# Retention and a gated two-layer product on one core: the queries of the sixth to eighth piece loaded as squares

## The chip, the cores and the metric

The kernel runs on one core of a Trainium2 chip. The metric is the device time of one execution in microseconds (us), and a kernel's time is the median of several executions. The engines are TensorE (PE: matmuls; PEld: the loading of their weights), VectorE (DVE), ScalarE (ACT), GpSimd (POOL) and SyncE (SP, which here only issues DMAs). Each engine works through its own instructions in the order in which the program gives them.

## The reference, cut to what matters

```python
# q, k, v: (B=8, H=8, S=576, D=64) float32; w_in (512, 2048), w_out (2048, 512) float64
scores = q @ k.transpose(0, 1, 3, 2) / sqrt(64)
gamma = 1 - 2.0 ** (-5 - arange(8))                     # one decay for each head
Dmat = where(i >= j, gamma ** (i - j), 0)               # i: query's place, j: key's place
ret = (scores * Dmat) @ v
x = ret.transpose(0, 2, 1, 3).reshape(4608, 512)
h = x @ w_in                                            # (4608, 2048)
out = (h * erf(softplus(h))) @ w_out                    # (4608, 512)
```

## The kernel before

**Pieces and chunks.** The 4608 tokens are cut into 36 pieces of 128 tokens (`pieces`). Nine pieces hold two sequences: four of the first, four of the second, and one with the last 64 tokens of both. Pieces are counted from 0 in the code, so the "sixth to eighth" are pieces 5, 6 and 7, the second to fourth piece of the second sequence. Four pieces (`PC = 4`) make a chunk of 512 tokens, and the two-layer product works on one chunk at a time.

**The retention of a piece** is three steps. `transposes(i)` brings the queries and keys into the form that TensorE needs, with the head's 64 dimensions on the partitions (`qT`, `kT`). `scores(i)` makes 8 products `s` of `kT` and `qT` (L347), which VectorE multiplies by the triangular mask into `sT` (L99, two instructions of 128x512). `outputs(i)` makes the outputs `o` from `sT` and the values (L365), adds what the sequence's running state gives (L376), and forms the new state from keys and values (L388). VectorE scales `o` into the chunk's operand `x` (L99), and the state is decayed (L427). The values are weighed by the keys' decay on GpSimd (`weigh_values`, L313).

**Two forms of loading.** `load_rows` reads a piece of q, k or v with tokens on the partitions, in two DMAs of 128 KB made of runs of 256 bytes (L147). Queries and keys loaded so are transposed by TensorE, four 128x128 transposes against `ident` into PSUM (L332), and copied out by ScalarE (L334 for q, L338 for k). `load_squares` reads a piece in four DMAs, one for each 32 partitions, with runs of 896 bytes (L131). VectorE then transposes all squares of 32x32 in one instruction (L326, `STREAM_TRANSPOSE`), with no TensorE and no ScalarE in it. Each of the four DMAs is 112 KB, because every run covers four tokens, of which half the dimensions are used. In the kernel before, queries are squares from piece 8 (`SQUARES = 2 * PC`) and keys from piece 12, unless the piece is one of those that need the keys with tokens on the partitions; those have rows of k as well.

**The weights** come as 64-bit floats. `round_weights` turns them into 32-bit floats part by part, four parts for the first group of `w_in` (`wa`): two steps on ScalarE (L254, L255), then six on VectorE (L259, L263, L267, L272, L274, L275) one behind the other; for other parts the last two are on GpSimd.

**The two-layer product** is made of products by 7 sums in place of 8 (`First`, `Second`), but for the first two chunks, whose first layer is made plainly (`plain`, L550: tiles `p`, `pe`, `pg`, which need the four parts of `wa` one after the other).

**Order.** Everything is put in order by hand. The beginning, with the first chunk's retention, the rounding and the first plain products, follows a string of letters: `a` is the next step of the retention, `p` a quarter of a plain product, a digit that many rounding steps, `w` the loading of a weight part, `k` two filler products.

```python
    keep_busy(10)
    ...
    for what in "alkakakawkakakawaa3awwa2aaa5ppappawwppa5ppapp5wawcppa5ppappaa5s":
```

Loads are issued ahead: `transposes(i)` ends with the queries of piece i + 2, and `outputs(i)` ends with keys and values of piece i + 3. All go to SyncE's queue, but the keys of piece 0, which go to ScalarE's. A tile framework puts a wait ahead of each instruction for what it reads and overwrites; its DMAs take 8 completion semaphores in turn, so a DMA is issued only after the one 8 places ahead of it has landed.

**Filler products.** `keep_busy(n)` issues n products of a tile with itself, whose result is not used: ten at the start, and two at each `k`. The tile is `ones`, which VectorE fills.

Of the kernel before, what the change touches and what calls it, by code (L numbers as in the profile page):

```python
# [11 lines left out]
FP32 = mybir.dt.float32  # L12
# [6 lines left out]
P = 128  # L19
# [35 lines left out]
def kernel(  # L55
# [10 lines left out]
    nc = tc.nc  # L66
# [15 lines left out]
    cpool = ctx.enter_context(tc.tile_pool(name="cpool", bufs=1))  # L82
# [18 lines left out]
    def flat(ap):  # L101
        return ap.rearrange("p h d -> p (h d)")

    heads = [slice(e * D, (e + 1) * D) for e in range(2)]
# [7 lines left out]
    PC = TCH // P  # L112
# [3 lines left out]

    SQUARES = 2 * PC
    SQUARES_K = 3 * PC  # L120
    SQ = 32

    def load_squares(i, name, src):
        t = raw.tile([P, NP, P * D // SQ], FP32, tag=name + "s", name=f"raw_{name}s", bufs=2)
        for b, s0, n, r0 in pieces[i]:
            m = n // SQ * D
            for part in range(P // SQ):
                e, d0 = part // 2, part % 2 * SQ
                tokens = src[b, e * NP : (e + 1) * NP, s0 : s0 + n, :].rearrange("p (r a) d -> r p (a d)", r=SQ)
                at = r0 // SQ * D  # L130
                nc.sync.dma_start(  # L131
                    out=t[part * SQ : (part + 1) * SQ, :, at : at + m - SQ], in_=tokens[:, :, d0 : d0 + m - SQ]
                )
        return t

    def load_rows(i, name, src, bufs):
        if name == "q":
            t = raw.tile([P, NP, P * D // SQ], FP32, tag="qs", name="raw_q", bufs=bufs)
            t = t.rearrange("p a x -> p (a x)")[:, : H * D].rearrange("p (h d) -> p h d", h=H)
        else:  # L140
            t = raw.tile([P, H, D], FP32, tag=name, name=f"raw_{name}", bufs=bufs)
        for b, s0, n, r0 in pieces[i]:
            for e in range(2):
                heads = src[b, e * NP : (e + 1) * NP, s0 : s0 + n, :]

                queue = nc.scalar if (name, i) == ("k", 0) else nc.sync
                queue.dma_start(out=t[r0 : r0 + n, e::2, :], in_=heads.rearrange("h p d -> p h d"))  # L147
        return t

    def load(i, names="qkv"):  # L150
        if i < len(pieces):
            t = loaded.setdefault(i, {})
            for name in names:
                src = {"q": q, "k": k, "v": v}[name]
                if name == "q" and i < SQUARES:
                    t["q"] = load_rows(i, "q", q, 2)
                elif name == "q":
                    t["qs"] = load_squares(i, "q", q)
                    if i >= SQUARES_K:
                        t["ks"] = load_squares(i, "k", k)  # L160
                elif name == "v" or i < SQUARES_K or len(pieces[i]) == 1:
                    t[name] = load_rows(i, name, src, 4)

    ones = cpool.tile([P, P], FP32, name="ones")
    nc.vector.memset(ones, 1.0)
    load(0)
    cst = cpool.tile([P, CONST_COLS], FP32, name="cst")
    nc.sync.dma_start(out=cst[:, :CONST_FIRST], in_=consts[:, :CONST_FIRST])
# [123 lines left out]
    ident = cpool.tile([P, P], FP32, name="ident")  # L292
# [21 lines left out]

    def transposes(i):
        t = live[i] = loaded.pop(i)
        if i < SQUARES:
            weigh_values(i)
        for name in "qk":
            tT = t[name + "T"] = att.tile([P, NP, P], FP32, tag=name + "T", name=name + "T")  # L320
            if name + "s" in t:
                for _, _, n, r0 in pieces[i]:
                    a = r0 // SQ * D
                    squares = t[name + "s"][:, :, a : a + n // SQ * D].rearrange("p h (a d) -> p h a d", d=D)
                    order = "p h (a r) -> p h a r" if name == "q" else "p h (r a) -> p h a r"
                    nc.vector.transpose(  # L326
                        out=tT[:, :, r0 : r0 + n].rearrange(order, r=SQ), in_=squares[:, :, :, :SQ]
                    )
            else:
                pt = ps_at.tile([P, NP, P], FP32, tag="at", name=f"pt_{name}")  # L330
                for p in range(NP):
                    nc.tensor.transpose(pt[:, p, :], flat(t[name][:, 2 * p : 2 * p + 2, :]), ident)  # L332
                if name == "q":
                    nc.scalar.copy(  # L334
                        out=tT.rearrange("p h (a r) -> p h a r", r=SQ), in_=pt.rearrange("p h (r a) -> p h a r", r=SQ)
                    )
                else:
                    nc.scalar.copy(out=tT, in_=pt)  # L338
        load(i + 2, "q")
# [14 lines left out]
    def outputs(i):  # L354
        segments = pieces[i]
        t = live.pop(i)
        seen = [(kept[b], r0, n) for b, s0, n, r0 in segments if s0 > 0]

        b, s0, n, _ = segments[0]
        o = [ps_at.tile([P, NP, P], FP32, tag="at", name=f"o{j}") for j in range(2)]
        for p in range(NP):
            for e in range(2):
                nc.tensor.matmul(  # L365
                    o[p % 2][heads[(e + p) % 2], p // 2, :],
                    lhsT=t["v"][:, 2 * p + e, :],
                    rhs=t["sT"][:, e, p, :],
                    start=(p < 2),
                    stop=(not seen and p >= NP - 2),  # L370
                    skip_group_check=True,
                )
        for state, r0, m in seen:
            for p in range(NP):
                for e in range(2):
                    nc.tensor.matmul(  # L376
                        o[p % 2][heads[(e + p) % 2], p // 2, r0 : r0 + m],
                        lhsT=state[heads[e], p, :],
                        rhs=t["qT"][heads[e], p, r0 : r0 + m],
                        start=False,  # L380
                        stop=(p >= NP - 2),
                        skip_group_check=True,
                    )
        if n == P:
            kv = flat(o[0])[:, 2 * P :].rearrange("p (a d) -> p a d", a=NP)
            for p in range(NP):
                for e in range(2):
                    nc.tensor.matmul(  # L388
                        kv[heads[e], p, :],
                        lhsT=t["k"][:, 2 * p + e, :],  # L390
                        rhs=t["v"][:, 2 * p + e, :],
                        start=False,
                        stop=(p == NP - 1),
                        skip_group_check=True,
                    )
        c, at = i // PC, i % PC * P
        if (0, c) not in x:
            x[0, c] = x_tile()

        def scaled(j):  # L400
            to = x[0, c][:, j:NP:2, at : at + P]
            if c < n_ch - 1:
                by = (gq if n == P else gq2)[:, j::2, :].unsqueeze(2).to_broadcast([P, 2, P // n, n])
                dst, got = (y.rearrange("p a (m i) -> p a m i", i=n) for y in (to, o[j][:, :2]))
                tt(dst, got, by, ALU.mult)
                return

            for r0 in range(0, P, n):
                dst = to[:, :, r0 : r0 + n].rearrange("p h (r a) -> p h a r", r=SQ)
                got, by = (  # L410
                    y.rearrange("p h (a r) -> p h a r", r=SQ)
                    for y in (o[j][:, :2, r0 : r0 + n], (gq if n == P else gq2)[:, j::2, :])
                )
                tt(dst, got, by, ALU.mult)

        scaled(1)
        if n == P:
            sums = kv
            if s0 > 0:
                sums = att.tile([P, NP, D], FP32, tag="sums", name="sums")  # L420
                tt(sums, kv, kept[b], ALU.add)

            if b % 2 == 0 and s0 + P + D == S:
                new = att.tile([P, NP, D], FP32, tag="last", name="last", bufs=1)
            else:
                new = att.tile([P, NP, D], FP32, tag="state", name="state")
            (nc.gpsimd if s0 > 0 else nc.vector).tensor_tensor(out=new, in0=sums, in1=gp, op=ALU.mult)  # L427
            kept[b] = new
        scaled(0)
        load(i + 3, "kv")  # L430
        if i + 1 >= SQUARES:
            weigh_values(i + 1)

    stages = [(transposes, 0), (scores, 0)]
# [271 lines left out]
    idle = ps_e.tile([P, W], FP32, tag="g", name="idle")  # L706

    def keep_busy(n):
        for _ in range(n):
            nc.tensor.matmul(idle[:, :P], lhsT=ones, rhs=ones, start=True, stop=True)  # L710


    most = [before_chunk(2)]
# [4 lines left out]
            attend(min(done[0] + stages, most[0]))  # L718
            round_weights(rounds[step] if step < len(rounds) else 0)

    keep_busy(10)
    weigh_values(0)
    products = firsts[0].plain()

# [36 lines left out]
    for b, nxt in zip(blocks[2:], blocks[3:] + [None]):  # L761
        n = order.index((b.g, b.c))
# [73 lines left out]
```

## Time and profile before

| | |
|---|---|
| median of 3 executions | 1028.51 us (1027.02 to 1029.08) |
| the profiled execution | 1028.51 us, of which the span of instructions is 1026.7 us |
| PE busy | 1017.5 us (99%), 6348 instructions |
| DVE busy | 669.2 us (65%) |
| ACT busy | 390.2 us (38%) |
| POOL busy | 123.5 us (12%) |
| the chain that ended last | PE 95%, DMA 2%, DVE 2% |
| DMA | 165.76 MB, mean 161 GB/s |
| granted TensorE clock | 1.00 |

Times in the trace are counted from the first instruction. A line such as `31.56 0.63 PE L332 MATMUL pt_q<-ident,raw_q ... x4 [0.24 <-DMA raw_q<-in_q_dram]` says: at 31.56 us TensorE began four instructions of line 332 that write `pt_q`; before them it had been idle for 0.24 us, until the DMA that writes `raw_q` landed. `SPq` lines are DMA issues on SyncE's queue. A TensorE instruction's duration includes its way through the array, and the next one starts earlier; the chain of waits shows the time that a group takes from the next.

### The profile page before, as it was taken

The page shows a single profiled execution, that of the slowest core. Times are in us where ns is not written, and L with a number is a line of the kernel's source. Part 1 is how long each engine was busy: PE and PEld are TensorE (multiplying, and loading weights), DVE is VectorE, ACT ScalarE, POOL GpSimd, SP SyncE. Part 2 cuts the span into 40 slices and gives each one's busy share as a digit, 9 for nine tenths or more (in the row PEclk, how much of TensorE's full clock was granted, in tenths as well). Part 3 has the DMA queues.
Part 4 walks back from the last instruction along what each step waited for, and adds up shares of the span by engine and source line. Part 5 has one row for each costly group of instructions (what it writes and reads, how often), then busy time and mean ns, then how long its engine had stood idle before and what let it go on. Part 6 is the DMA issues. An engine that isn't in the chain of part 4 may idle for free.

```text
span 1026.7 us, 15951 instructions
## 1 busy us (share of the span) xinstructions
PE 1017.5 (99%) x6348; PEld 876.0 (85%) x6348; DVE 669.2 (65%) x1055; ACT 390.2 (38%) x481; POOL 123.5 (12%) x122
## 2 busy tenths in 40 slices
PE   9999999999999999999999999999999999999998
PEld 8778888888788888888888888888888888888887
DVE  3868777877876666656666666666567655555555
ACT  2254134233134444434443344444443333333332
POOL 2143112122312110010001001000100000000000
PEclk9999999999999999999999999999999999999999
DMA  9999889979974344544445345444433334444333
GB/s 197 190 240 195 224 199 222 250 153 245 237 183 161 128 144 144 168 162 160 154 150 170 123 144 157 170 146 144 144 124 124 123 131 131 126 133 135 124 91 115
DMA packets 146986, 165.76 MB, mean 161 GB/s; under 512 B 97376, under 2 KB 121568, under 8 KB 138848
## 3 DMA queue, kind: packets, MB, share of 16 engines
q1 hardware_dynamic: 144848, 163.70, 56.3%
q10 hardware_dynamic: 2064, 1.05, 0.4%
q8 instruction: 50, 0.82, 0.4%
q14 instruction: 24, 0.20, 0.1%
HBM read 117.52 MB, written 47.19 MB: 160 GB/s over the span
## 4 chain that ended last, share of the span: by engine, by line
PE 95%; DMA 2%; DVE 2%; SPq 0%; issue 0%; ACT 0%; DVEq 0%
PE a L604 24%; PE a L496 23%; PE g L604 12%; PE g L496 12%; PE e L604 6%; PE e L496 6%; PE s L347 3%; PE o L365 3%; PE o L388 1%; PE o L376 1%; DMA raw_k<-in_k_dram 1%; PE p L550 1%; PE idle L710 1%; DMA wraw<-in_moe_w_out_dram 1%; PE pg L550 1%; PE pe L550 1%
## 5 line engine op out<-in xcount | busy, mean ns | idle before, releaser
L496 PE MATMUL a<-x,wa 128*128 128x256 f32 x1088 | 258.3, 380 | 0.0
L496 PEld LDWEIGHTS a<-x,wa 128*128 128x128 f32 x1088 | 205.7, 190 | 28.5
L604 PE MATMUL a<-wb,s 128*128 128x256 f32 x864 | 205.7, 381 | 0.0
L604 PEld LDWEIGHTS a<-wb,s 128*128 128x128 f32 x864 | 162.9, 190 | 23.6 <-ACT o L618 0.7
L99 DVE TENSOR_TENSOR t<-g,t 128x512 f32<-128x512 f32 x68 | 47.0, 691 | 150.9 <-ACT t L526 113.3
L496 PE MATMUL g<-x,wa 128*128 128x256 f32 x544 | 129.2, 380 | 0.0
L496 PEld LDWEIGHTS g<-x,wa 128*128 128x128 f32 x544 | 102.8, 190 | 14.4
L99 DVE TENSOR_TENSOR o<-a,o 128x512 f32<-128x512 f32 x108 | 74.1, 686 | 49.3 <-PE a L604 49.3
L521 ACT COPY t<-a 128x512 f32<-128x512 f32 x34 | 19.9, 586 | 188.2 <-PE a L496 188.2
L99 DVE TENSOR_TENSOR t<-t,s 128x1024 f32<-128x1024 f32 x72 | 89.4, 1282 | 0.0
L565 ACT ACTIVATE s<-t 128x1024 f32<-128x1024 f32 x72 | 72.2, 1049 | 27.3 <-DVE t L99 27.3
L274 POOL TENSOR_TENSOR wraw<-wraw 128x512 f32<-128x512 f32 x28 | 29.5, 1052 | 435.8 <-DVE wraw L272 187.0
L99 DVE TENSOR_TENSOR x<-x 128x512 f32<-128x512 f32 x115 | 75.8, 693 | 1.2
L532 ACT COPY t<-a 128x512 f32<-128x512 f32 x34 | 19.9, 587 | 144.4 <-PE a L496 144.4
L569 ACT ACTIVATE s<-s 128x1024 f32<-128x1024 f32 x72 | 72.1, 1049 | 0.4
L604 PE MATMUL g<-wb,s 128*128 128x256 f32 x288 | 68.6, 381 | 0.0
L604 PE MATMUL e<-wb,t 128*128 128x256 f32 x288 | 68.5, 380 | 0.0
L604 PE MATMUL a<-wb,t 128*128 128x256 f32 x288 | 68.5, 380 | 0.0
L604 PE MATMUL g<-wb,t 128*128 128x256 f32 x288 | 68.2, 380 | 0.0
L99 DVE TENSOR_TENSOR sT<-s,cst 128x512 f32<-128x512 f32 x72 | 46.2, 682 | 31.6 <-PE s L347 31.5
L99 DVE TENSOR_TENSOR o<-g,o 128x512 f32<-128x512 f32 x72 | 49.2, 684 | 24.5 <-ACT o L618 19.7
L496 PE MATMUL e<-x,wa 128*128 128x256 f32 x272 | 64.8, 381 | 0.0
(76 smaller groups left out, 1225.5 us busy)
## 6 DMA issues: line engine op xcount, KB each, us to landing
od<-o SPq DMA_DIRECT2D x54, 512.0 KB, 3.3
x<-xd SPq DMA_DIRECT2D x27, 1024.0 KB, 4.8
o<-od SPq DMA_DIRECT2D x27, 1024.0 KB, 5.3
raw_qs<-in_q_dram SPq DMA_DIRECT2D x96, 112.0 KB, 4.7
raw_ks<-in_k_dram SPq DMA_DIRECT2D x84, 112.0 KB, 4.1
xd<-x SPq DMA_DIRECT2D x9, 1024.0 KB, 5.2
raw_v<-in_v_dram SPq DMA_DIRECT2D x64, 128.0 KB, 4.7
wraw<-in_moe_w_in_dram SPq DMA_DIRECT2D x32, 256.0 KB, 5.9
```

The source lines that it names most:

```text
L99: nc.vector.tensor_tensor(out=out, in0=in0, in1=in1, op=op)
L274: engine.tensor_tensor(out=r_f, in0=high_f, in1=r_f, op=ALU.mult)
L347: nc.tensor.matmul(ps[e][:, p, :], lhsT=t["kT"][heads[e], p, :], rhs=t["qT"][heads[e], p, :], start=True, stop=True)
L365: nc.tensor.matmul(o[p % 2][heads[(e + p) % 2], p // 2, :], lhsT=t["v"][:, 2 * p + e, :], rhs=t["sT"][:, e, p, :], start=(p < 2), stop=(no ...
L376: nc.tensor.matmul(o[p % 2][heads[(e + p) % 2], p // 2, r0 : r0 + m], lhsT=state[heads[e], p, :], rhs=t["qT"][heads[e], p, r0 : r0 + m], s ...
L496: nc.tensor.matmul(acc[:, j * TH : (j + 1) * TH], lhsT=weights["wa", self.g][:, a, d, j * P : (j + 1) * P], rhs=x[self.g, self.c][a][:, d, :],
L521: nc.scalar.copy(out=self.t1[:, 1], in_=self.a)
L532: nc.scalar.copy(out=self.t2[:, 0], in_=self.a)
L550: nc.tensor.matmul(acc[n][:, j * TH : (j + 1) * TH], lhsT=wa[:, slots[f], dc % 2, j * P : (j + 1) * P], rhs=t[:, dc, tok * TH : (tok + 1) ...
L565: nc.scalar.activation(self.s[:, j], t, AF.Softplus)
L569: nc.scalar.activation(self.s[:, j], self.s[:, j], AF.Erf)
L604: nc.tensor.matmul(acc[:, tp, :], lhsT=left[:, j * TH + tp * P : j * TH + (tp + 1) * P], rhs=weights["wb", self.g][:, b, j, :], start=(sta ...
```

## The change

Queries become squares from piece 5 instead of piece 8 (keys as before from piece 12). The keys of piece 0 go to SyncE's queue, between the queries and the values of piece 0. The tile `ones` is gone: the filler products use `ident`, which GpSimd makes, and the first series has nine instead of ten. The two other uses of `SQUARES`, which say when the values are weighed, are written as `2 * PC` and keep their value.

```diff
-    SQUARES = 2 * PC
+    SQUARES_Q = PC + 1
     SQUARES_K = 3 * PC
...
-
-                queue = nc.scalar if (name, i) == ("k", 0) else nc.sync
-                queue.dma_start(out=t[r0 : r0 + n, e::2, :], in_=heads.rearrange("h p d -> p h d"))
+                nc.sync.dma_start(out=t[r0 : r0 + n, e::2, :], in_=heads.rearrange("h p d -> p h d"))
...
-                if name == "q" and i < SQUARES:
+                if name == "q" and i < SQUARES_Q:
                     t["q"] = load_rows(i, "q", q, 2)
...
-    ones = cpool.tile([P, P], FP32, name="ones")
-    nc.vector.memset(ones, 1.0)
...
-        if i < SQUARES:
+        if i < 2 * PC:
             weigh_values(i)
...
-        if i + 1 >= SQUARES:
+        if i + 1 >= 2 * PC:
             weigh_values(i + 1)
...
-            nc.tensor.matmul(idle[:, :P], lhsT=ones, rhs=ones, start=True, stop=True)
+            nc.tensor.matmul(idle[:, :P], lhsT=ident, rhs=ident, start=True, stop=True)
...
-    keep_busy(10)
+    keep_busy(9)
```

Line numbers after the change are lower by 2 to 4: the DMA of rows moves from L147 to L145, TensorE's transposes from L332 to L328, VectorE's from L326 to L322, the scores from L347 to L343, the masked scores stay on L99, the outputs move from L365 to L361, the plain product from L550 to L546.

## The prediction

> **What bounds the kernel now.** First the page, the share of each engine:
>
> ```profile
> PE 1017.5 (99%) x6348; PEld 876.0 (85%) x6348; DVE 669.2 (65%) x1055; ACT 390.2 (38%) x481; POOL 123.5 (12%) x122
> ```
>
> TensorE is busy 99% of the span, so a change is worth what it takes from TensorE's own work, less the idle time that it makes. Second, TensorE's waits over the whole span, to see how little there is:
>
> ```profile
> PE idle L710 <- DVE ones L165: 1.1, 1, 1.1
> PE s L347 <- DVE kT L326: 0.9, 1, 0.9
> PE o L365 <- POOL raw_v L313: 0.8, 1, 0.8
> PE p L550 <- DVE wa L275: 0.7, 1, 0.7
> PE pt_k L332 <- DMA raw_k<-in_k_dram: 0.7, 2, 0.4
> ```
>
> All but the second lie in the first 70 us, where the change is. Third, therefore, TensorE's timeline around pieces 5 and 6:
>
> ```profile
> 29.32 1.99 PE L550 MATMUL p<-x,wa 128*128 128x256 f32 x8
> 31.56 0.63 PE L332 MATMUL pt_q<-ident,raw_q 128*128 128x128 f32 x4 [0.24 <-DMA raw_q<-in_q_dram]
> 32.63 0.63 PE L332 MATMUL pt_k<-ident,raw_k 128*128 128x128 f32 x4 [0.44 <-DMA raw_k<-in_k_dram]
> ...
> 46.21 0.60 PE L332 MATMUL pt_q<-ident,raw_q 128*128 128x128 f32 x4
> 46.64 0.60 PE L332 MATMUL pt_k<-ident,raw_k 128*128 128x128 f32 x4
> 47.08 1.03 PE L550 MATMUL pe<-x,wa 128*128 128x256 f32 x4
> 47.95 1.03 PE L550 MATMUL pg<-x,wa 128*128 128x256 f32 x4
> 48.90 1.16 PE L347 MATMUL s<-qT,kT 64*128 64x128 f32 x16
> ```
>
> Piece 5 waits for its loads: TensorE runs here as fast as the DMAs allow. Piece 6 waits for nothing. Fourth, VectorE's timeline over the same time:
>
> ```profile
> 39.52 1.29 DVE L99 TENSOR_TENSOR sT<-s,cst 128x512 f32<-128x512 f32 x2 [2.24 <-PE s L347]
> 40.73 0.42 DVE L259 TENSOR_SCALAR wa<-wa 128x512 f32<-128x512 f32 x1
> ...
> 45.23 0.79 DVE L259 TENSOR_SCALAR wa<-wa 128x512 f32<-128x512 f32 x1
> ...
> 49.22 0.69 DVE L275 TENSOR_TENSOR wa<-wa,wraw 128x512 f32<-128x512 f32 x1
> 50.09 1.29 DVE L99 TENSOR_TENSOR sT<-s,cst 128x512 f32<-128x512 f32 x2 [0.18 <-PE s L347]
> ```
>
> From the masked scores of piece 5 (39.52) to the end of the last rounding step (49.22 + 0.69 = 49.91), VectorE has no gap: sT, the third part of `wa`, three scalings, the fourth part. It has 65% of the span, but none to spare here.
>
> **The change, part by part.** The sum is made on the profiled execution: 1028.51 us, 1.8 of it outside the span of 1026.7; it is also the median, so differences carry over unchanged.
>
> *TensorE's transposes go.* Three groups of four. The chain of waits has each at 0.44 us (`46.37 0.44 PE pt_q L332 x4`), so 3 x 0.44 = 1.32 us less work. ScalarE loses three copies of 0.59 us; no wait of TensorE's in pieces 5 to 7 names them, so that is worth nothing.
>
> *Piece 5: the keys come later.* Two DMAs of 128 KB become four of 112 KB: 4 x 114.7 - 2 x 131.1 = 197 thousand bytes more, ahead of the keys in SyncE's queue. Stretches in which one kind fills the queues give the price per byte:
>
> ```profile
> core 0: us, PE busy (x) PEld busy (x) DVE busy (x) ACT busy (x) POOL busy (x), PEclk, DMA share, GB/s
> 9.00:13.00 4.00, 4.00 (x54) 3.57 (x53) 2.14 (x5) 1.13 (x2) 1.05 (x1) 1.00 1.37 218
> 76.00:79.00 3.00, 3.00 (x17) 2.48 (x15) 2.96 (x6) 0.59 (x1) 0.00 (x0) 1.00 1.15 221
> ```
>
> Rows (9 to 13 us) move at 218 GB/s, squares (76 to 79) at 221: no difference, so the extra bytes cost 197/218 = 0.9 us. The chain of waits has the keys' last DMA as what releases TensorE (`26.09 6.40 DMA raw_k<-in_k_dram`, landing at 32.49); they would land at 33.4. TensorE, with nothing left between `p` and the keys, idles from 31.3 to 33.5, and everything behind it, masked scores and VectorE's chain included, is 0.9 us late. The 0.44 us saved on this piece vanishes in that wait. Bounds: 0 if the extra bytes find unused DMA time, 1.6 if they move as slowly as the mixed traffic of 24 to 28 us (126 to 202 GB/s in the slices of the DMA view, 197/126 = 1.6). I take 0.9, the row of the same kind of load.
>
> The Trainium skill, "DMA: Bandwidth & Descriptors", Specifications, asks for at least 512 bytes per run for full rate, which favours squares: were the rows' 218 GB/s half of the full rate, four squares would take 459/436 = 1.05 us against 1.2 for two row DMAs, the keys would be 0.15 us early and the whole change would come to about +1.3 us. The two stretches above speak against that here.
>
> *Piece 6: the queries stand behind the rounding.* In the built program the transpose of `qT` for piece 6 is VectorE's next instruction after the last L275 of the fourth part, and the scores of piece 6 wait for it. Before, they started at 48.90 while VectorE was still rounding until 49.91. After: 49.91 + 0.9 (lateness of piece 5) + 0.70 for the transpose (the groups by shape: `L326 DVE STREAM_TRANSPOSE qT<-raw_qs 128x512 ... x4 | 2.8, 702`) + 0.04 for the hand-over = 51.55, which is 2.65 us after 48.90. TensorE would arrive at 48.90 + 0.9 - 0.44 = 49.36 and idle 2.2 us, the transposes' saving again swallowed. Queued behind the transpose is only sT of piece 6, which needs those scores anyway. Bounds for the transpose: 0.70 to 1.14 (the one kT transpose in the first 100 us, beside GpSimd).
>
> *Piece 7: here the saving stays.* Its transpose stands after four rounding steps of `wb` and ahead of the scalings; VectorE would have it done by about 57.5 and TensorE wants it at 56.76 + 2.2 = 59.0. No wait: -0.44.
>
> *What comes behind.* The wait of 0.8 us for `raw_v` at 58.74 (piece 7's values, behind the rounding on GpSimd) moves with VectorE's rounding by about 1.5 us, less than TensorE's 2.2, so it shrinks; but the same outputs also wait for sT's second half at 59.25, which moves with the scores. Nothing is gained. After that TensorE waits for nothing of weight, so the lateness stays to the end.
>
> *The start.* The filler products begin after GpSimd's `ident` (end 1.30) instead of VectorE's `ones` (end 1.00): 0.3 later, one product (0.43) less, so -0.1 for the first transposes. SyncE issues two more DMAs (0.5 us each) before the values and the constants, but the DMA queues fill from 2 us on, so the landings shift by 0 to 0.2 us. ScalarE loses two issues and starts its table load earlier, off the path. Piece 5 waits for DMAs whatever came before, so only the shift of the landings counts: +0.1.
>
> *SyncE's queue:* 6 more issues of about 0.43 us. The row DMAs are held up there anyway (the values of piece 5 took 2.99 and 1.42 us to issue), and squares have a quarter of the descriptors each; nothing added, 0 to 0.9 kept for the range.
>
> Sum: 0.1 + 0.9 + 1.75 (2.65 - 0.9) - 0.44 = +2.3 us: 1028.5 + 2.3 = 1030.8. A measurement of this kernel tells about 0.2%, 2.06 us, from nothing; the line is at 1030.57.
>
> **The rivals.**
>
> *The keys are not late (the other side).* Where the DMA queue has room between 24 and 31 us, piece 5's keys land by 32.5 as before. For: the four squares leave fewer descriptors, and the stretch moved only 168 GB/s. Against: its DMA share is 1.21, the queues are never empty. Then 0.1 + 1.75 - 0.44 = +1.4, 1029.9, no measurable change. It decides if the keys come less than 0.65 us later.
>
> *The bytes of all three pieces count.* Pieces 6 and 7 bring 0.9 us more each, and the debt reaches the keys of piece 9, at 68 us the next load for which TensorE waits. Against: the 2.2 us lateness gives the loads that much more time. Then up to +1.8 more: 1032.6.
>
> *TensorE's clock falls back* in the two idle times of 2.2 us. The granted clock is 1.00 in every row, but the first 20 filler records take 4.64 us and later groups of 4 about 0.45, so the array starts at half speed, for 5.2 us. No row shows a pause over 0.9 us after that. If it happened once: half of 5.2 = 2.6 more, 1033.4. The Trainium skill, "TensorE: Matmul & The Clock Gate", HAM oscillation, puts the limit at idle gaps of about 3.4 us; by that nothing would be added.
>
> *A gain:* if VectorE reached piece 6's queries in time and the keys were not late, -1.3 - 0.1: 1027.1. The order on VectorE excludes it unless its chain is 2 us shorter.
>
> **How the numbers follow.** Forecast 0.58, own range 1030.1 to 1031.7 (0.42 of it above the line, 0.16 below). Keys not late 0.14 (same). All three pieces 0.12, clock 0.10 (slower). Gain 0.06. So slower 0.42 + 0.12 + 0.10 = 0.64, same 0.16 + 0.14 = 0.30, faster 0.06. The range goes from 1028.8 (the first rival less about half the spread of the runs before, 1.0) to 1033.0; outside are the gain and most of the clock case.
>
> **What would show it.** Right: TensorE idle about 2 us before `pt_k` of piece 5 (released by `raw_k`), and about 2 us before the scores of piece 6, released by VectorE's `qT`; TensorE's work 1.3 us less; nothing else moved after 70 us. Wrong: no wait on `qT`; the keys of piece 5 before 33 us; filler-like spacing (0.21 us) behind one of the pauses; a wait at piece 9's keys of over 1 us.

## The result

The change makes the kernel slower: 1033.18 us, the median of 6 runs (1030.1 to 1036.5), against 1027.33 in 6 runs of the kernel before beside it (1026.85 to 1029.08). The ratio is 1.0053, with a 95% interval of 1.0033 to 1.0074. The prediction was 1030.8 and slower. The profiled execution took 1033.0 us, of which 1031.2 us is span, 4.5 us more than the profiled execution of before; by the medians the difference is 5.9 us, because the six runs of before beside it are a little faster than that one.

The page of the kernel after, share of each engine:

```profile
PE 1016.9 (99%) x6334; PEld 875.3 (85%) x6334; DVE 670.5 (65%) x1057; ACT 389.1 (38%) x478; POOL 122.6 (12%) x122
```

TensorE has 14 instructions less (12 transposes, and the two that make up one filler product), ScalarE 3 copies less. The busy time fell by 0.6 us where 1.32 of work went; that alone says little, since two traces of the kernel before differ by 1.1 us in it, but the timeline below shows work that was stretched. Its waits over the whole span (engine, line and tile that waited, what it waited for; us in total, times, longest):

```profile
PE pt_k L328 <- DMA raw_k<-in_k_dram: 2.6, 2, 2.0
PE s L343 <- DVE qT L322: 2.2, 1, 2.2
PE s L343 <- DVE kT L322: 1.4, 1, 1.4
```

These three are new in this size, and the first two are the ones that the prediction named. Their places, in TensorE's timeline of the kernel after:

```profile
33.93 0.63 PE L328 MATMUL pt_k<-ident,raw_k 128*128 128x128 f32 x4 [2.03 <-DMA raw_k<-in_k_dram]
...
48.80 1.03 PE L546 MATMUL pg<-x,wa 128*128 128x256 f32 x4
51.98 1.16 PE L343 MATMUL s<-qT,kT 64*128 64x128 f32 x16 [2.15 <-DVE qT L322]
53.07 3.47 PE L546 MATMUL p<-x,wa 128*128 128x256 f32 x8
```

Piece 5 waits 2.03 us for its keys, and piece 6 waits 2.15 us for its queries' transpose. The last line is the surprise: eight products of `p` take 3.47 us, where eight of them took 1.99 in the timeline of before (at 29.32). VectorE's timeline shows why piece 6 waits:

```profile
50.52 0.69 DVE L271 TENSOR_TENSOR wa<-wa,wraw 128x512 f32<-128x512 f32 x1
51.13 0.70 DVE L322 STREAM_TRANSPOSE qT<-raw_qs 128x512 f32<-128x512 f32 x1
53.15 1.29 DVE L99 TENSOR_TENSOR sT<-s,cst 128x512 f32<-128x512 f32 x2 [1.31 <-PE s L343]
```

The transpose follows on the heels of the last rounding instruction, as predicted; then it is VectorE that waits, for the scores. The slow `p` is explained by the view in stretches of time (busy time of each engine, then the granted clock, the DMA share and the rate):

```profile
core 0: us, PE busy (x) PEld busy (x) DVE busy (x) ACT busy (x) POOL busy (x), PEclk, DMA share, GB/s
52.00:53.00 1.00, 1.00 (x16) 0.95 (x16) 0.00 (x0) 0.58 (x2) 0.00 (x0) 1.00 1.10 316
54.00:55.00 1.00, 1.00 (x3) 0.79 (x3) 0.97 (x3) 0.13 (x1) 0.00 (x0) 0.50 0.49 99
57.00:58.00 1.00, 1.00 (x7) 0.90 (x6) 0.03 (x1) 0.76 (x2) 0.92 (x2) 1.00 0.97 370
```

After the pause the granted clock fell from 1.00 to 0.50. The trace's clock record has the fall at 53.43 us and the rise at 56.84, so 3.41 us at half speed, which costs half of that, 1.7 us. Before, the record stays at 1.00 from 6.28 us to the end of the work. The third wait lies far behind the change, again in TensorE's timeline of after:

```profile
238.84 1.16 PE L343 MATMUL s<-qT,kT 64*128 64x128 f32 x16 [1.39 <-DVE kT L322]
```

VectorE itself had waited 2.57 us there for the DMA of `raw_ks`. In the kernel before, the same scores (piece 27) start without any wait:

```profile
233.50 1.16 PE L347 MATMUL s<-qT,kT 64*128 64x128 f32 x16
```

**Where the 4.5 us are.** The start of each piece's scores in one trace against that in the other gives the lateness, in us: 1.30 at piece 5, 3.08 at piece 6 (+1.78), 4.33 at piece 7 (+1.69 for the clock, -0.44 for the transposes that are gone), 3.89 at piece 9, and unchanged until piece 26; 5.34 at piece 27 (the wait for `kT`), 4.37 at piece 31 (where before had its own wait of 0.9 for `kT`, which after has not), and 4.5 at the end.

### The profile page after: what moved, and what is told of

It is laid out like the page before. It is cut to its first block, busy times and chain, and to the rows that moved or that the text cites. A ratio compares the mean times of both kernels' runs of the same rounds, so it can differ in the third digit from the quotient of the medians.

```text
span 1031.2 us, 15926 instructions
## 1 busy us (share of the span) xinstructions
PE 1016.9 (99%) x6334; PEld 875.3 (85%) x6334; DVE 670.5 (65%) x1057; ACT 389.1 (38%) x478; POOL 122.6 (12%) x122
## 4 chain that ended last, share of the span: by engine, by line
PE 92%; DMA 4%; SPq 2%; DVE 1%; issue 0%; DVEq 0%
PE a L600 24%; PE a L492 22%; PE g L600 12%; PE g L492 11%; PE e L600 6%; PE e L492 6%; PE s L343 3%; PE o L361 3%; PE o L384 1%; PE o L372 1%; DMA raw_k<-in_k_dram 1%; DMA wraw<-in_moe_w_in_dram 1%; DMA raw_qs<-in_q_dram 1%; PE p L546 1%; SPq L145 1%; SPq L131 1%
## 5 line engine op out<-in xcount | busy, mean ns | idle before, releaser
L99 DVE TENSOR_TENSOR t<-g,t 128x512 f32<-128x512 f32 x68 | 46.9, 690 | 150.9 <-ACT t L522 113.1
L99 DVE TENSOR_TENSOR o<-a,o 128x512 f32<-128x512 f32 x108 | 74.2, 687 | 49.3 <-PE a L600 49.3
L99 DVE TENSOR_TENSOR t<-t,s 128x1024 f32<-128x1024 f32 x72 | 88.0, 1262 | 0.0
L99 DVE TENSOR_TENSOR x<-x 128x512 f32<-128x512 f32 x115 | 75.7, 692 | 1.2
L99 DVE TENSOR_TENSOR sT<-s,cst 128x512 f32<-128x512 f32 x72 | 46.2, 682 | 33.6 <-PE s L343 33.6
L99 DVE TENSOR_TENSOR o<-g,o 128x512 f32<-128x512 f32 x72 | 49.3, 684 | 24.3 <-ACT o L614 19.5
```

The lines of the kernel that those rows point to most:

```text
L99: nc.vector.tensor_tensor(out=out, in0=in0, in1=in1, op=op)
```

## The experiments

The theory after the result: the change costs the two waits (keys and `qT`), 3.1 us, and the fall of the clock that the second brings, 1.7. First rival: it is the start that costs. Second rival: it is the added bytes (three pieces, 590 thousand bytes, 2.7 us of DMA time at 218 GB/s), which come due wherever TensorE waits for loads, so that mending the waits brings nothing. The table has the medians, the ratio to the kernel before run beside them, and the lateness in the traced run at the scores of some pieces. The last two rows are single runs.

| kernel | median us (runs) | ratio (95%) | 5 | 6 | 7 | 9 | 27 | 31 |
|---|---|---|---|---|---|---|---|---|
| after | 1033.18 (6) | 1.0053 (1.0033-1.0074) | 1.30 | 3.08 | 4.33 | 3.89 | 5.34 | 4.37 |
| squares_only | 1032.57 (5) | 1.0039 (1.0027-1.0051) | 1.27 | 3.05 | 2.61 | 2.81 | 5.62 | 5.21 |
| start_only | 1029.05 (12) | 1.0006 (0.9998-1.0014) | 0.73 | 0.73 | 0.73 | 1.66 | 2.10 | 3.38 |
| fill_both | 1031.98 (5) | 1.0033 (1.0020-1.0046) | 1.57 | 3.35 | 2.92 | 2.48 | 4.71 | 5.40 |
| from_piece7 | 1028.52 (11) | 1.0002 (0.9994-1.0011) | 0.03 | 0.03 | -0.41 | 0.43 | 0.43 | -0.56 |
| early_qT6 | 1032.49 (5) | 1.0035 (1.0022-1.0048) | 1.34 | 0.90 | 1.16 | 0.73 | 2.78 | 3.75 |
| keys_first | 1033.22 (5) | 1.0046 (1.0034-1.0058) | -0.40 | 1.51 | 2.70 | 2.84 | 4.51 | 4.60 |
| both_mended | 1032.47 (5) | 1.0041 (1.0029-1.0053) | -0.04 | -0.11 | 0.72 | 2.53 | 3.68 | 3.84 |
| five_and_seven | 1031.51 (7) | 1.0031 (1.0020-1.0042) | -0.54 | -0.27 | 0.70 | 2.13 | 2.97 | 2.95 |
| extra_bytes | 1030.74 (7) | 1.0029 (1.0018-1.0041) | 0.32 | 0.32 | 0.32 | 2.10 | 3.20 | 3.40 |
| split_rows | 1028.41 (11) | 1.0003 (0.9994-1.0011) | -0.23 | -0.23 | -0.23 | -0.10 | -0.10 | 0.41 |
| before_again | 1027.07 (1) | | 0.00 | -0.01 | -0.01 | -0.45 | -0.45 | -1.43 |
| early_again | 1033.92 (1) | | 1.64 | 1.20 | 1.41 | 1.63 | 4.86 | 5.29 |

The kernel before itself, run beside these, had medians of 1028.28 (beside squares_only to from_piece7), 1028.61 (early_qT6 to five_and_seven) and 1028.19 (the rest). A single trace can lie over 1 us from its median, so the lateness tells where, and the medians tell how much.

**squares_only**: the kernel before with squares from piece 5; start, queues and filler products as before.

```diff
-    SQUARES = 2 * PC
+    SQUARES_Q = PC + 1
...
-                if name == "q" and i < SQUARES:
+                if name == "q" and i < SQUARES_Q:
```

> The start as before (keys of piece 0 on ScalarE's queue, ten filler products of ones); queries as squares from piece 5. If the two waits and the clock behind them are the cause: a wait of 1.5 to 2.1 us at the keys of piece 5, of 2.1 to 2.2 us at the queries of piece 6, TensorE's scores of piece 7 about 2.2 us later than before without a fall of the clock and 3.9 with one; 2 to 5 us over the kernel before. If the start is the cause (rival): within 1 us of the kernel before.

TensorE's timeline of squares_only:

```profile
33.89 0.63 PE L332 MATMUL pt_k<-ident,raw_k 128*128 128x128 f32 x4 [1.68 <-DMA raw_k<-in_k_dram]
51.95 1.16 PE L347 MATMUL s<-qT,kT 64*128 64x128 f32 x16 [2.15 <-DVE qT L326]
53.04 1.99 PE L550 MATMUL p<-x,wa 128*128 128x256 f32 x8
```

Both waits come from the squares alone, at the same places within 0.05 us. The clock did not fall in this traced run (`p` takes 1.99 again, and piece 7 is 0.44 less late than piece 6, the saving in full). Yet at piece 31 the lateness is 5.21: 2.6 us came later, the largest part as a wait of 1.81 us for `kT` at 239 us. So even without a fall of the clock the two waits and the saving are not the whole.

**start_only**: the kernel after, with queries as squares only from piece 8.

```diff
-    SQUARES_Q = PC + 1
+    SQUARES_Q = 2 * PC
```

> The changed start alone; queries are rows until piece 8, as before. If the waits of pieces 5 and 6 are the cause: the keys of piece 1 land about 1 us later, the keys of piece 5 0.3 to 0.6 us later, no other wait appears, the clock stays at 1.0: 0 to 0.6 us over the kernel before. If the start is the cause (rival): 3 to 5 us over it.

No difference that can be told (1.0006). The start as the cause falls. Its traced run was the slowest of its twelve (1027.55 to 1031.9), so the lateness in its row is that of one such run.

**fill_both**: the kernel after, with filler products into a PSUM tile that is overwritten next, one series ahead of `pt_k` of piece 5, one ahead of the scores of piece 6.

```diff
+                if (name, i) == ("k", 5):
+                    for _ in range(8):
+                        nc.tensor.matmul(pt[:, 0, :], lhsT=ident, rhs=ident, start=True, stop=True)
...
+        if i == 6:
+            for _ in range(8):
+                nc.tensor.matmul(ps[0][:, 0, :], lhsT=ident, rhs=ident, start=True, stop=True)
```

> The changed kernel with eight filler products (1.7 us) ahead of the transposes of piece 5's keys and eight ahead of the scores of piece 6, into PSUM that the real work overwrites: TensorE waits as long, but is busy. If the clock falls because TensorE pauses: no stretch at half clock, the waits keep their ends, the time is 1.7 us or more below the changed kernel, about 2.6 us over the kernel before, and the runs lie closer together than 1030 to 1036. If the clock has nothing to do with the pause (rival): as the changed kernel, 5 to 6 us over the kernel before.

TensorE's timeline of fill_both:

```profile
49.94 1.95 PE L346 MATMUL s<-ident 128*128 128x128 f32 x16
52.26 1.16 PE L349 MATMUL s<-qT,kT 64*128 64x128 f32 x16 [0.37 <-DVE qT L322]
53.35 1.99 PE L552 MATMUL p<-x,wa 128*128 128x256 f32 x8
```

With the pause filled, the scores come no earlier, but the clock holds there and `p` takes 1.99: piece 7 is 2.92 late instead of 4.33. By itself this does not prove that the pause is the cause, since the clock held in squares_only's traced run too, with the pause left open; the last section has what speaks for it. But 2.5 us come back later: a wait of 1.92 for `kT` with half clock behind it, in this run at 239 us. By the medians the gain is not settled, since the intervals of fill_both and after overlap.

**from_piece7**: squares_only with squares from piece 7 only.

```diff
-    SQUARES_Q = PC + 1
+    SQUARES_Q = PC + 3
```

> The start as before; of pieces 5 to 7 only piece 7 has its queries as squares. If my step for piece 7 holds (its transpose on VectorE is done before TensorE needs it): no wait on qT, no fall of the clock, TensorE 0.44 us ahead from piece 7 on: 0 to 0.6 us below the kernel before, too little to tell apart in the times but plain in the trace. If squares cost in themselves, by their DMAs or VectorE (rival): 0.5 us or more over it, with a later landing of the weights or keys that follow.

Piece 7 keeps its 0.44 us, with no wait (lateness 0.03 at piece 6, -0.41 at piece 7), as the prediction had it. But piece 9 is already 0.43 late, and the median is that of before. One piece's saving and one piece's bytes may cancel; sums this small are not to be told from chance here, since the second trace of before has moved by 0.45 at piece 9.

**early_qT6**: the kernel after, with the transpose of piece 6's queries moved ahead of the rounding steps.

```diff
         for name in "qk":
+            if name + "T" in t:
+                continue
...
         scaled(0)
+        if i == 5:
+            t6 = loaded[6]
+            t6["qT"] = att.tile([P, NP, P], FP32, tag="qT", name="qT")
+            nc.vector.transpose(
+                out=t6["qT"].rearrange("p h (a r) -> p h a r", r=SQ),
+                in_=t6["qs"].rearrange("p h (a d) -> p h a d", d=D)[:, :, :, :SQ],
+            )
         load(i + 3, "kv")
```

> The changed kernel with the transpose of piece 6's queries put on VectorE ahead of the last part's rounding instead of behind it. If the place in VectorE's order is the cause of the second wait: no wait on qT, the first plain product behind the scores of piece 6 waits about 1.1 us for the rounding instead, which ends 0.7 later; TensorE is 1.9 us late there instead of 3.1, 1.5 at piece 7, no half clock: about 1.5 to 2 us over the kernel before, 3 below the changed one. If the transpose waits for its DMAs rather than for its turn (rival): the wait on qT and the fall of the clock stay, 5 us over.

TensorE's timeline of early_qT6:

```profile
49.80 1.16 PE L345 MATMUL s<-qT,kT 64*128 64x128 f32 x16
51.59 1.99 PE L555 MATMUL p<-x,wa 128*128 128x256 f32 x8 [0.63 <-DVE wa L271]
```

The wait for `qT` is gone, and with it the fall of the clock in the 50s. The rounding behind it is 0.7 us later and now releases `p`, but 2.2 us are won at piece 6 (0.90 late instead of 3.08). At the end only a little of it is left: the lateness grows from 0.73 at piece 9 to 3.75 at piece 31, by waits for `kT`, one of which was followed by half clock. The median, 1032.49, is not to be told from squares_only's.

**keys_first**: the kernel after, with piece 5's keys and values issued ahead of its queries.

```diff
-        load(i + 2, "q")
+        if i + 2 != 5:
+            load(i + 2, "q")
...
         load(i + 3, "kv")
+        if i + 3 == 5:
+            load(5, "q")
```

> The changed kernel with the four DMAs of piece 5's queries issued behind the keys and values of piece 5 instead of ahead of them. If the extra bytes ahead of the keys are the cause of the first wait: the keys land by 32.5 instead of 33.8, the wait at them falls from 2.0 to under 1 us, the scores of piece 5 within 0.5 us of the kernel before; the second wait of 2.1 us stays, with the half clock in some of the runs: 1.3 to 3.3 us over the kernel before. If the keys are late for another reason (the start, SyncE's issues; rival): the wait stays near 2 us.

TensorE's timeline of keys_first:

```profile
31.84 0.63 PE L328 MATMUL pt_k<-ident,raw_k 128*128 128x128 f32 x4 [0.30 <-DMA raw_k<-in_k_dram]
50.41 1.60 PE L344 MATMUL s<-qT,kT 64*128 64x128 f32 x16 [2.02 <-DVE qT L322]
```

The keys come 0.79 us earlier than before the change and the wait for them is down to 0.30 us (0.44 before the change); piece 6's is still 2.02, and the clock fell again after it. So it was the loads ahead of the keys that made them late, not the start, which this kernel has as well. The median is not better than after's.

**both_mended**: early_qT6 and keys_first in one.

> The changed kernel with both edits: piece 5's queries behind its keys, piece 6's transpose ahead of the last rounding. If the two waits are the whole loss: the scores of piece 5 as before within 0.5 us, the plain product behind piece 6 waits about 1.1 us, piece 7 within 0.5 us of the kernel before, no half clock; the time 0 to 0.8 us over the kernel before. If squares cost by a third way (rival): 2 us or more over it.

TensorE's timeline of both_mended:

```profile
57.48 1.16 PE L346 MATMUL s<-qT,kT 64*128 64x128 f32 x16 [0.51 <-DVE qT L324]
60.31 1.16 PE L364 MATMUL o<-sT,raw_v 128*64 128x128 f32 x16 [1.67 <-POOL raw_v L309]
...
70.61 0.63 PE L330 MATMUL pt_k<-ident,raw_k 128*128 128x128 f32 x4 [1.64 <-DMA raw_k<-in_k_dram]
```

This run settles the main question. Up to piece 6 TensorE is on time (-0.11), both predicted waits are gone, the clock has not fallen in this traced run, and the median is still 0.41% above the kernel before. The debt appears at the next loads. The values of piece 7 had landed at 52.60 us; what held up the outputs at 60 us is that GpSimd weighs them behind its rounding, and the rounding begins with ScalarE's step on the first part of `w_out`. ScalarE's timelines, of before and of both_mended, and GpSimd's of both_mended:

```profile
51.87 0.68 ACT L254 ACTIVATE wb<-wraw 128x512 f32<-128x512 f32 x1 [3.89 <-DMA wraw<-in_moe_w_out_dram]
53.93 0.67 ACT L250 ACTIVATE wb<-wraw 128x512 f32<-128x512 f32 x1 [6.11 <-DMA wraw<-in_moe_w_out_dram]
59.20 1.05 POOL L309 TENSOR_TENSOR raw_v<-raw_v,cst 128x512 f32<-128x512 f32 x1
```

That part of the weights landed 2.06 us later (53.90 against 51.84). Behind it come the keys of piece 9 at 70.6 us, and `kT` later.

**five_and_seven**: squares for pieces 5 and 7 and rows for piece 6, with the start of before and the keys of piece 5 first.

```diff
-    SQUARES = 2 * PC
+    SQUARES_Q = PC + 1
...
-                if name == "q" and i < SQUARES:
+                if name == "q" and (i < SQUARES_Q or i == 6):
...
-        load(i + 2, "q")
+        if i + 2 != 5:
+            load(i + 2, "q")
...
+        if i + 3 == 5:
+            load(5, "q")
```

> The start as before; queries as squares for pieces 5 and 7 (piece 6 stays rows), piece 5's queries behind its keys. If my account of all three pieces holds: no wait on qT, the keys of piece 5 at 32.0 or earlier, TensorE 0.3 to 0.7 us ahead at the scores of piece 5 and 0.8 to 1.1 ahead from piece 7 on: 0.8 us under the kernel before, at the edge of what the times can tell. If VectorE's or the DMAs' extra work counts (rival): nothing gained, 0 to 1 us over it.

A clear miss: 1.0031, slower. Until piece 6 it is ahead of before (-0.27), and then the loads are late. VectorE's timeline shows it:

```profile
54.61 0.43 DVE L259 TENSOR_SCALAR wb<-wb 128x512 f32<-128x512 f32 x1 [3.50 <-ACT wb L254]
```

ScalarE's rounding step, for which VectorE waits 3.50 us, waited for the first part of `w_out`, which landed at 53.87 us, as late as in both_mended. The same wait on VectorE is 0.46 us in from_piece7. The clock was halved once too, from 60.8 us on. The transpose for piece 7 stands in VectorE's order behind these rounding steps and came late too.

**extra_bytes**: the kernel before, all queries as before, and behind the values of pieces 5, 6 and 7 two more DMAs of 96 KB each into a tile that nobody reads: the same 197 thousand bytes a piece that squares add.

```diff
+                if name == "v" and 5 <= i < 8:
+                    b, s0, n, _ = pieces[i][0]
+                    for e in range(2):
+                        heads = q[b, e * NP : e * NP + 3, s0 : s0 + n, :]
+                        nc.sync.dma_start(out=scratch[:, e], in_=heads.rearrange("h p d -> p h d"))
...
+    scratch = cpool.tile([P, 2, 3, D], FP32, name="scratch")
```

> The kernel before, with two more DMAs behind the values of pieces 5, 6 and 7 that load 196.6 KB of queries into a tile that nothing reads: the extra bytes and issues of the squares without their transposes and without a delay of the keys of piece 5. If the bytes and issues of the loads make the late waits for kT at 200 to 275 us: those waits grow by 1 to 3 us, 1 to 3 us over the kernel before. If those waits come from TensorE's lateness or from chance (rival): within 0.6 us of the kernel before.

TensorE's waits in extra_bytes:

```profile
PE o L371 <- POOL raw_v L319: 1.9, 1, 1.9
PE pt_k L338 <- DMA raw_k<-in_k_dram: 1.9, 3, 0.9
PE s L353 <- DVE kT L332: 1.9, 2, 1.0
```

ScalarE's timeline of extra_bytes:

```profile
53.78 0.68 ACT L260 ACTIVATE wb<-wraw 128x512 f32<-128x512 f32 x1 [5.49 <-DMA wraw<-in_moe_w_out_dram]
```

With no change at all in the work of TensorE and VectorE, and with piece 5's keys only 0.32 us later, the loads alone make the kernel slower: 1.0029 (1.0018 to 1.0041), 2.5 us, close to the 2.7 us of DMA time of their bytes. The waits are of the kind that both_mended had, the first part of `w_out` included (it landed at 53.76). The clock did not fall in the traced run; in two of the seven its mean is lower (0.996 and 0.998), and the five others have a median of 1030.40, still 2.2 us above the kernel before. One difference to squares remains: these bytes come in runs of 256, so they add packets as well, where a piece of squares takes half as many packets as a piece of rows. That it is bytes that count rests on the two forms moving at the same rate.

**split_rows**: the kernel before, with each of the two row DMAs of pieces 5 to 7's queries cut in two: as many issues as squares need, and not a byte more.

```diff
+                if name == "q" and 5 <= i < 8:
+                    for r in range(0, n, n // 2):
+                        nc.sync.dma_start(
+                            out=t[r0 + r : r0 + r + n // 2, e::2, :],
+                            in_=heads[:, r : r + n // 2, :].rearrange("h p d -> p h d"),
+                        )
+                    continue
```

> The kernel before, with the queries of pieces 5 to 7 still as rows but in four DMAs of 64 KB instead of two of 128: six more issues on SyncE, no byte more. If the number of issues on SyncE's queue makes the late waits: 1 to 3 us over the kernel before, with SyncE's loads later and later from 100 to 230 us. If the bytes do, or TensorE's lateness: within 0.6 us of the kernel before.

1.0003 (0.9994 to 1.0011): nothing that can be told. The issues on SyncE's queue are free here; the bytes are not.

**before_again** and **early_again**: the kernel before and early_qT6, one run each, to see how much a single trace of the same kernel moves.

> The kernel before once more, for a second trace of it. If the loads' timing between 100 and 275 us varies by chance by some us from run to run: the values of a piece at 228 us are issued up to 2 us earlier or later than in the first trace, and the wait of 0.9 us for kT moves or goes. If it is the same each time: within 0.3 us of the first trace at every piece.

> The kernel with piece 6's transpose moved ahead, once more, for a second trace. If its late waits (3.7 us at 200 to 275 us in the first trace, of which 1.7 is half clock) are its own: again 1.5 us or more there. If they are chance: under 1 us in the one or the other.

The second trace of before is 1.4 us shorter than the first and has no wait for `kT`, where the first had 0.9. The second trace of early_qT6 has two such waits, 3.9 us together, where the first had 2.2. So these late waits are partly chance, but they grow with the added bytes: in the four traces without a byte more (before, before_again, start_only, split_rows) VectorE's `kT` keeps TensorE waiting for 0 to 1.3 us in all, in the nine with the bytes of two or three pieces more for 1.4 to 3.9.

**The clock, run by run.** One window at half clock, 3.41 us, takes 1.7 us, and with it the mean granted clock of a run to 0.998 or lower; so the runs can be sorted by it. In after, five of six runs are at 0.995 to 0.998 (1031.92 to 1036.5 us), and the one at 0.999 took 1030.1. In after, squares_only and fill_both, which have the same loads, the seven runs at 0.999 or more lie 3.1 us above the median of before beside them, and the nine others 5.7 (medians). In early_qT6, keys_first and both_mended the nine runs at 0.999 or more lie 3.9 above it: with one or both waits mended and the clock up, nothing is gained.

No kernel that was tried beats the kernel before; from_piece7, split_rows and start_only are not to be told from it.

## Why the prediction was right, and where it was wrong

- **Direction and mechanism: right.** Both predicted waits stand where they were put, with the releaser that was named.
- **Keys of piece 5: right kind, too small.** Predicted 1.0 us of lateness at piece 5 (0.1 and 0.9), measured 1.30, and 1.27 without the new start. Five traces with these loads have 1.27 to 1.64, so the term was sized 0.3 to 0.6 us too small. It lies within the 0 to 1.6 that was kept open. The rule of 512 bytes a run in the Trainium skill, "DMA: Bandwidth & Descriptors", Specifications, did not show: the kernel after moves rows (9 to 13 us) at 222 GB/s and squares (76 to 79 us) at 224. The 75% more bytes of a square were not made up for by longer runs.
- **Queries of piece 6: right.** Predicted +1.75 and scores at 51.55; measured +1.78 and 51.98, the 0.4 being that of the keys.
- **Piece 7: right.** -0.44 in squares_only and in from_piece7.
- **The start: wrong at its own place, without effect that can be told.** Loads were to land 0 to 0.2 us later; the keys of piece 1 landed 0.97 later (10.63 against 9.66), and piece 1's scores were 0.96 late. By piece 4 it was 0.58. start_only's one trace, its slowest run, is 0.73 late at piece 5, where 0.1 was predicted, but this does not add to the squares' 1.27, and start_only's median shows no cost.
- **SyncE's issues: right.** Costed at nothing, and split_rows measures nothing.
- **The clock: a rival, given 0.10 and no term in the sum, came true.** This is the larger step that failed. The fall cost 1.7 us in the traced run instead of the 2.6 estimated from the 5.2 us at the start, and five of after's six runs have a clock that low. In the one that has not, after is 2.8 us above the kernel before, near the 2.3 of the sum.
- **"After that TensorE waits for nothing of weight": wrong.** This is the other step that failed. The bytes of pieces 6 and 7 were a rival with 0.12, on the reason that TensorE's 2.2 us of lateness gives the loads that much time. In after's own trace the reason nearly held: the keys of piece 9 landed 0.59 us later (68.54 against 67.95), and what the loads behind piece 7 did, with both signs, comes to nothing (4.33 late at piece 7, 4.37 at piece 31). But where the waits are mended the lateness that was to pay for the bytes is gone, and they cost 2.2 us or more: with the bytes alone added, or with keys and queries mended, the waits come at 60, at 70 and between 235 and 280 us. The prediction also had the first of these places wrong: not the keys of piece 9, but the first part of `w_out`, on which the weighing of piece 7's values hangs.

So the sum was 2.3 us and the traced difference 4.5: 0.3 from the keys, 1.7 from the clock, and little from all loads behind piece 7. The median, 1033.18, lies 0.2 above the range given, and the traced execution, 1033.0, at its end. That early_qT6, keys_first and both_mended won so little back is best explained by the stream of loads, which over the first 300 us is nearly as long as TensorE's path: mend the waits on TensorE's path, and the stream sets the end. This is argued from the runs above and from the DMA's rows of the kernel before, not measured by itself:

```profile
core 0: us, PE busy (x) PEld busy (x) DVE busy (x) ACT busy (x) POOL busy (x), PEclk, DMA share, GB/s
60.00:100.00 40.00, 39.75 (x399) 32.33 (x396) 31.96 (x55) 18.89 (x25) 13.40 (x12) 1.00 1.01 231
100.00:140.00 40.00, 40.00 (x371) 32.63 (x371) 29.19 (x47) 10.93 (x14) 7.90 (x9) 1.00 0.79 197
300.00:340.00 40.00, 40.00 (x294) 33.83 (x289) 29.54 (x51) 14.58 (x20) 8.52 (x8) 1.00 0.49 173
```

The DMA share is 0.79 to 1.01 from 60 to 300 us and falls to 0.49 behind that. At 0.79 the queues are not full all the time (a stretch that one kind of load fills has 1.15 to 1.37), so room was left there. But the loads also follow the engines: between 100 and 240 us of the kernel before SyncE waits 6.4 us for VectorE's `qT` alone ahead of loads of squares, whose buffers come free that way, and so loads that fell behind with the engines need not catch up.

What stays open besides: between 100 and 220 us the values in the traces with two or three pieces' added bytes fall another 1 to 4 us behind those of before, while TensorE falls at most 0.9 further behind, and no run tells why. The four runs of both_mended with the clock up lie 2.5 to 4.4 us above the kernel before, more than the 2.2 of the bytes alone; whether VectorE's three added transposes, or chance, make the difference was not tested.

## What to carry to other kernels

When two resources both run near full over a stage, price a change on each of them, from its own rows, up to the point where the resource has slack again; a form of loading that spares an engine 1.3 us and reads 75% more bytes is a bad trade where the loads are nearly the limit. An instruction moved to an engine with 65% of load may still land behind the one stretch in which that engine has no gap: look at its order there, not at its share. And a pause of TensorE can cost more than its length, so its neighbours' durations are to be looked at as well.

## What the runs showed of the hardware

The granted clock fell after a pause of only 2.15 us. The fall at 53.43 us lies 14 times 3.413 us behind the first rise at 5.644, and the half clock lasted 3.413 us. In keys_first the fall lies 13 times as far behind the rise, in five_and_seven 16 times, in early_qT6 and fill_both 68 times: the decision is taken at the edges of fixed windows. The Trainium skill, "TensorE: Matmul & The Clock Gate", Part 1, has such a free-running window of 3.4 us, which agrees; its limit for a pause, an idle window of about 3.4 us, does not, and the measurement decides.

In the window ahead of its fall TensorE was busy for 42% in after; the four other falls came at 41, 42, 44 and 49%, while windows of 43, 44, 47 and 51% saw none. In the two traces of before no window behind the start has less than 72%, and the clock did not fall until the work ended. This is why the pause, and not chance, is taken to bring the fall. After's first pause, 2.03 us long, was cut in two by an edge (69 and 71% busy), and nothing fell. So where a pause lies against the edges matters as well as its length, but the exact limit is not settled by these runs. Half speed for one window cost half of it, 1.7 us, almost as much as the pause.
